# Taps of the last chunk on two DMA queues, step sizes and the sine's table first, and new figures for the order of the work: a gated attention and state-space kernel

## The chip, the cores and the metric

The kernel runs on one core of a Trainium2 chip. The core has a matmul engine (TensorE, PE in the profile), an engine for functions by table (ScalarE, ACT), a vector engine (VectorE, DVE), a general engine (GpSimd, POOL), and SyncE (SP), which here only starts DMA transfers. Each engine works through its own list of instructions in order and waits on semaphores that others raise. The metric is the time of one execution on the device in microseconds, the median of the runs.

## The reference

Two branches read the same x (2048 rows of 448), and a gate per row mixes them:

```python
g = sigmoid((x * gate_w).sum(-1, keepdims=True))
# A: attention with 16 query heads of 28, one key head and one value head
scores = einsum("bhqd,bkd->bhqk", q, k) * (28 ** -0.5)
a = einsum("bhqk,bkd->bhqd", softmax(scores), v) ... @ wo
# B: a long convolution with taps from 256 complex modes per channel
dt = exp(log_dt)[:, None]
P = exp(dt * (A_re + 1j*A_im) * l)            # l = 0..2047
K = einsum("dn,dnl,dn->dl", Cc, P, dt * Bc).real
b = causal_convolution(x, K) + x * Dskip      # by FFT in the reference
return g * a + (1 - g) * b
```

## The kernel before, in words

**Attention.** The 16 groups of work (four query blocks of 512 rows by four groups of four heads) each meet 16 key blocks, which makes 1024 score tiles of 128x512. They are taken in sets of three and two by turns: TensorE writes scores into PSUM (L1289 by row groups of 29, L1312 with a zero-padded query in qM; in the last 64 tiles L1300 and L1303), ScalarE takes one exponential over the set (L1344), and TensorE multiplies by the values (L1362, L1356). After each group the sums are copied out (L1127), the denominators go through DRAM, and four output projections per query block (L1109) are folded into O (L1118). For the last query block the end is different: two halves, each with a matmul that adds O through the identity (L1209), four projections (L1205) and a copy (L1226, L1223) before its store.

**Convolution.** The 448 channels are taken in 14 chunks of 32. For each, VectorE builds powers of the modes in a table by doubling (products L950, sums and differences L965, the closing products L979, a sign L986), TensorE turns the table into taps (L1009, two halves of a chunk), VectorE copies each half to `kstg` (L1019), and four DMAs on GpSimd's queue write it to DRAM (`KP_scratch`). SyncE loads the taps back as a Toeplitz pattern (`T`, four DMAs per eight channels), TensorE convolves (L1071), VectorE weights by 1-g (L1080), TensorE turns the result (L1091), and VectorE adds it to O (L1100). The input u of the convolution is rearranged from O's memory once, by 16 GpSimd copies (L598), and then shifted by DMAs.

**The start.** x comes in four blocks (`lx`) on SyncE's queue. Each block is transposed on TensorE (L639), copied from PSUM by ScalarE or VectorE (L649, L653), and multiplied by the key weights (L661); ScalarE writes kT (L673). The step sizes `log_dt` are one row, loaded on ScalarE's queue as the second DMA, spread over the partitions by a matmul with ones (L768), and taken through the exponential (L770), which is ordered behind the first copy of x. A dummy sine (L678) brings the sine's table in after the third block's copy; two real sines (L798, L799) and a dummy exponential (L800) follow.

**What sets the order.** A planner in the kernel's Python (`Prog.schedule`) places every operation by a planned duration in nanoseconds, a priority `pr` (smaller goes first among those that are ready), and the ends of what it depends on. It writes one order for each engine, and that order is what the chip follows. Durations are written at each operation: `el(n, rate)` is 68 + n/rate. `LAZY` adds a margin to matmuls of certain priorities; `PORT` holds VectorE for 0.55 of a long GpSimd operation. Transfers have planned costs too (`DMA_NS`, `iss`, `extra`). `pg.after` adds an order without data.

The planned durations of the exponentials, the table products and the folds are these:

```python
AF.Exp, scale=SQ), 58 + 512 * n / 1.2, rd=bk, wr=ew, pr=0)      # L1346, n = 3 or 2
def vo(fn, n, rd, wr, rate=1.92): ... el(n, rate)               # L930
ALU.mult, ALU.add), el(n), ...                                  # L1118, rate 0.96
```

Of the kernel before, what the change touches and what calls it, by code (L numbers as in the profile page):

```python
# [12 lines left out]
P = 128  # L13

S = 2048
D = 448
# [26 lines left out]
GATE = (30, 35)  # L43
WARM = 64
NEWQ = 15
STORES = (401, 405, 408)
# [38 lines left out]
class Prog:  # L85
# [12 lines left out]
    LAZY = {1.2: 200.0, 1.4: 200.0, 1.55: 200.0, 1.6: 200.0}  # L98
# [303 lines left out]
class Kernel:  # L402
# [75 lines left out]
    def consts(self):  # L478
# [21 lines left out]
        for k in range(2):  # L500
            pm(V(self.qM, k * XQ, XQ), 0.0, 1800, [("qM", k)], 1.5)
# [15 lines left out]
    def loads(self):  # L517
# [12 lines left out]
        def lraw(k, eng="sp"):  # L530
# [5 lines left out]
        lx(0)  # L536
        pg.dma([(wks.v(0, DT, 0, [[1, 112]]), dram(ins["A_wk"], 0, [[112, DT], [1, 112]]))], (112, 224), "wk", wr=["wks"], eng="act")
        pg.dma([(self.dtb.v(0, 1, 0, [[1, D]]), dram(ins["B_log_dt"], 0, [[D, 1], [1, D]]))], (1, 896), "ldt", wr=["dt"], eng="act")
        lx(1)
        pg.dma([(wks.v(0, DT, 112, [[1, 112]]), dram(ins["A_wv"], 0, [[112, DT], [1, 112]])),  # L540
                (wks.v(0, DT, 224, [[1, 4]]), dram(ins["gate_w"], 0, [[4, DT], [1, 4]]))],
               (224, 200), "wv", wr=["wvs"], eng="act", extra=1500)
# [4 lines left out]
               (112, 3584), "wq", wr=["wqs"], fac=0.85)  # L547
        lraw(1)
# [5 lines left out]
              180, rd=["wvs"], wr=["Wv"], pr=0.1)  # L554
        pg.op("dve", lambda e: e.tensor_copy(self.Wv.v(0, DT, 28, [[32, 4]]), wks.v(0, DT, 224, [[1, 4]])),
              100, rd=["wvs"], wr=["Wvg"], pr=0.1)
# [28 lines left out]
    def prep_u(self):  # L585
        pg = self.pg
        done = []
        for half in range(2):
            for k in range(2):
                for j in range(0, 8, 2):  # L590
                    jj = 8 * k + j
                    if half == 0:
                        dst, w = self.U.v(0, P, 2 * jj, [[128, UA // 2], [1, 4]]), ["Uz", ("Ub", k)]
                    else:
                        dst, w = self.T.v(0, P, UB + 2 * jj, [[32, UA // 2], [1, 4]]), ["rawdone", ("UB", k)]
                    key = ("ustd", half, jj)
                    done.append(key)
                    pg.op("pool", lambda e, dst=dst, jj=jj, half=half: e.tensor_copy(  # L598
                        dst, self.O.v(0, P, jj * D + half * UA, [[2, UA // 2], [D, 2], [1, 2]])), 660,
                        rd=[("ust", k)] + ([] if half else []), wr=w + [key], pr=1 + half)  # L600
# [23 lines left out]
    def prep_x(self):  # L624
# [6 lines left out]
        for q in range(4):  # L631
            for hp in range(2):
# [15 lines left out]
                if hp == 0 or q == 3:  # L648
                    o = pg.op("act", lambda e, d=dst, s=src: e.activation(d, s, AF.Copy), 1000, rd=[("b", b)], wr=[key])  # L649
                    if q == 0:  # L650
                        self.xc0 = o.i
# [802 lines left out]
```

## Time and profile before

| | us |
|---|---|
| median of 3 runs | 502.0 (500.86 to 503.79) |
| the profiled execution | 503.36 |
| its span, first to last instruction | 501.5 |
| ScalarE busy | 485.0 |
| PE busy | 468.2 |
| VectorE busy | 455.7 |
| GpSimd busy | 166.5 |

The span is what the profile's rows cover; the profiled execution's time is 1.9 us longer. A row of the timeline gives start, duration, engine, line, operation, the tiles written and read, and in brackets the idle time before it and what ended it. Neighbouring instructions of a kind are merged, and the first form is the one shown. Instructions on one engine overlap by about 0.1 us, so the distance between two starts is what one costs. A wait's three numbers are the total, the count and the longest. Line numbers are those of the kernel before.

### The profile page before, as it was taken

Reading aid. Unit: us, or ns where it says so; the run is one execution under the profiler, and the core shown is the slowest. Engines: PE = TensorE matmul, PEld = TensorE weight load, DVE = VectorE, ACT = ScalarE, POOL = GpSimd, SP = SyncE. Lnnn points to the kernel's source line nnn. Section 1 sums busy time; section 2 is a strip of 40 time slices with the busy share of each in tenths; the row PEclk is TensorE's granted clock in tenths of the full one; section 3 lists DMA queues with packets and bytes.
Section 4 is the critical chain, followed back from the end, with each engine's and each line's share of the span. In section 5 each row is a group of like instructions: output and inputs, shape, how many; then the busy total and the mean of one; then the engine's idle time right before and its main releaser. Section 6 shows DMA issues by size and latency. Waiting matters only on the chain.

```text
span 501.5 us, 17468 instructions
## 1 busy us (share of the span) xinstructions
PE 468.2 (93%) x7651; PEld 213.7 (43%) x7734; DVE 455.7 (91%) x862; ACT 485.0 (97%) x435; POOL 166.5 (33%) x308
## 2 busy tenths in 40 slices
PE   8899999999999999989999999988999999999997
PEld 6532233344443334444443434434444253455563
DVE  5999999999999999999999999989999999994222
ACT  5999999999999999999999999989999999999995
POOL 5106534233243243224316124521512540535110
PEclk9799999999999999999999999989999999999999
DMA  8997289847519348995934861799692666777942
GB/s 236 324 190 191 26 189 132 274 118 241 158 25 284 102 125 208 276 242 114 272 87 104 237 180 46 225 250 263 175 255 36 195 205 182 218 204 209 298 153 78
DMA packets 151527, 91.86 MB, mean 183 GB/s; under 512 B 83514, under 2 KB 147436, under 8 KB 151452
## 3 DMA queue, kind: packets, MB, share of 16 engines
q1 hardware_dynamic: 141962, 81.05, 60.2%
q0 software_dynamic: 8960, 9.54, 7.8%
q8 instruction: 60, 0.98, 0.8%
q10 hardware_dynamic: 530, 0.17, 0.2%
q14 instruction: 15, 0.12, 0.1%
HBM read 73.61 MB, written 5.23 MB: 157 GB/s over the span
## 4 chain that ended last, share of the span: by engine, by line
DVE 57%; ACT 23%; PE 16%; DMA 2%; issue 1%; SPq 0%
ACT expT L1344 22%; DVE tab L950 19%; DVE tab L965 10%; DVE tab L979 4%; DVE tmp L973 3%; DVE msq L896 3%; PE psS L1289 2%; DVE kstg L1019 2%; PE psB L1362 2%; PE psS L1312 2%; DVE cst L1080 2%; DMA T<-KP_scratch 1%; DVE seedz L898 1%; DVE mbf L916 1%; DVE acc L1127 1%; DVE qT L869 1%
## 5 line engine op out<-in xcount | busy, mean ns | idle before, releaser
L1344 ACT ACTIVATE expT<-psS 128x1536 bf16<-128x1536 f32 (+1 forms) x410 | 466.2, 1326 | 4.6 <-PE psS L1289 2.8
L950 DVE TENSOR_TENSOR tab<-tab,mbf 128x512 bf16<-128x512 bf16 (+4 forms) x140 | 140.4, 1007 | 0.0
L1289 PE MATMUL psS<-qT,kT 29*128 29x512 bf16 x654 | 92.2, 387 | 8.1 <-ACT expT L1344 4.0
L1362 PE MATMUL psB<-expT,vaug 128*32 128x512 bf16 x960 | 96.1, 391 | 0.4 <-DVE acc L1127 0.3
L151 POOL DMA_DIRECT2D KP_scratch<-kstg x112 | 61.6, 557 | 101.5 <-DVE kstg L1019 101.0
L1312 PE MATMUL psS<-qM,kT 128*128 128x512 bf16 x234 | 76.1, 383 | 11.8 <-issue 8.1
L965 DVE TENSOR_TENSOR tab<-tab 128x256 bf16<-128x256 bf16 (+4 forms) x140 | 78.6, 585 | 0.0
L1362 PEld LDWEIGHTS psB<-expT,vaug 128*32 128x32 bf16 x960 | 24.6, 93 | 70.6 <-issue 68.8
L1271 PE MATMUL psB<-ident,one 128*128 128x512 bf16 x168 | 53.9, 383 | 0.1
L151 POOL DMA_DIRECT2D qM<-qT x64 | 32.6, 515 | 58.5 <-DVE qT L869 37.2
L1289 PEld LDWEIGHTS psS<-qT,kT 29*128 29x128 bf16 x654 | 22.6, 91 | 55.9 <-ACT expT L1344 40.8
L151 POOL DMA_DIRECT2D rdenB<-R_scratch x60 | 30.3, 510 | 48.1 <-DMA R_scratch<-denT 48.0
L1071 PE MATMUL psS<-T,U 128*26 128x128 bf16 (+3 forms) x1792 | 40.0, 223 | 0.7 <-DMA T<-KP_scratch 0.7
L1071 PEld LDWEIGHTS psS<-T,U 128*26 128x26 bf16 (+3 forms) x1792 | 31.6, 106 | 15.0 <-issue 9.6
L1071 PE MATMUL psX<-T,U 128*32 128x128 bf16 (+3 forms) x1472 | 33.8, 222 | 1.5 <-issue 1.2
L979 DVE TENSOR_TENSOR tab<-tab,tmp 128x1984 bf16<-128x1984 bf16 x28 | 32.6, 1188 | 0.1
L1071 PEld LDWEIGHTS psX<-T,U 128*32 128x32 bf16 (+3 forms) x1472 | 25.4, 106 | 14.1 <-issue 10.9
L1312 PEld LDWEIGHTS psS<-qM,kT 128*128 128x128 bf16 x306 | 18.8, 97 | 26.6 <-ACT expT L1344 17.0
L973 DVE TENSOR_TENSOR tmp<-tmp,mq 128x64 bf16<-128x64 bf16 (+4 forms) x70 | 26.1, 373 | 0.2
L1271 PEld LDWEIGHTS psB<-ident,one 128*128 128x128 bf16 x168 | 15.2, 97 | 23.0 <-issue 13.1
L896 DVE TENSOR_TENSOR msq<-seedz 128x512 f32<-128x512 f32 (+1 forms) x40 | 24.9, 622 | 0.0
L151 POOL DMA_DIRECT2D R_scratch<-denT x15 | 8.5, 565 | 48.1 <-DVE denT L1133 20.1
(186 smaller groups left out, 522.3 us busy)
## 6 DMA issues: line engine op xcount, KB each, us to landing
T<-KP_scratch SPq DMA_DIRECT2D x204, 272.0 KB, 5.0
U<-KP_scratch SPq DMA_DIRECT2D x20, 272.0 KB
rdenB<-R_scratch POOLq DMA_DIRECT2D x60, 64.0 KB
U<-cst SPq DMA_DIRECT2D x1, 3584.0 KB, 23.8
qM<-qT POOLq DMA_DIRECT2D x64, 32.0 KB, 4.6
tab<-in_A_x_dram SPq DMA_DIRECT2D x4, 448.0 KB, 6.1
O<-in_A_x_dram SPq DMA_DIRECT2D x16, 112.0 KB, 2.9
O<-cst SPq DMA_DIRECT2D x1, 1792.0 KB, 10.6
```

The costliest lines, as they stand in the source:

```text
L151: return [e.dma_start(o, i, **kw) for o, i in pairs]
L896: pg.op("dve", lambda e: e.tensor_tensor(m2(msq), z2, z2, ALU.mult), el(2 * n), rd=[kr, ki] + first, wr=["msq"], pr=pr)
L950: mul = lambda e, o, a, b: e.tensor_tensor(o, a, b, ALU.mult)
L965: vo(lambda e, dv=dv, tv=tv, k=k: e.tensor_tensor(dv, dv, tv, ALU.add if k else ALU.subtract), n, [kt[k], kd[k]], [kd[k]])
L973: vo(lambda e, w=w, lv=lv: e.tensor_tensor(rho.v(0, P, (32 - 2 * w) * 2, [[64, 32], [2, w], [1, 2]]), rho.v(0, P, (32 - w) * 2, [[64, 32], ...
L979: vo(lambda e, k=k: e.tensor_tensor(tab.v(0, P, FM + k * FP + 2, [[64, 32], [2, 31], [1, 2]]), tab.v(0, P, lm + k * PL + 62, [[64, 32], [- ...
L1071: r = e.matmul(ps.v(32 * j, 32 - m0, 128 * k, [[1, 128]]), self.U.v(0, P, (4 * gi + j) % UA // 2 * 128 + 2 * (2 * m0 + par) + j % 2, [[4, ...
L1271: return e.matmul(t.v(0, P, off, [[1, 512]]), self.one.v(0, P, 2, [[0, P]]), self.ident.v(0, P, 0, [[0, 4], [1, P]]), start=b != 6, stop=b ...
L1289: r = e.matmul(self.psS.v(0, P, 512 * b, [[1, 512]]), kT.v(32 * h, DH + 1, 128 * kt, [[1, 128]]), qT.v(32 * h, DH + 1, 512 * (i % 2), [[1, ...
L1312: return e.matmul(self.psS.v(0, P, 512 * b, [[1, 512]]), kT.v(0, P, 128 * kt, [[1, 128]]), self.qM.v(0, P, (i % 2) * XQ + 512 * h, [[1, 51 ...
L1344: pg.op("act", lambda e: e.activation(expT.v(0, P, 512 * es[0], spread(es, n)), self.psS.v(0, P, 512 * bs[0], spread(bs, n)), AF.Exp, scal ...
L1362: r = e.matmul(self.psB.v(32 * h, 32, 0, [[1, 512]]), vaug.v(0, P, 32 * kt, [[1, 32]]), expT.v(0, P, 512 * ring[t], [[1, 512]]), start=(kt ...
```

## The change

It has these parts.

- The last chunk (c = 13, `LASTQ`): the four DMAs that write the first half's taps go on SyncE's queue, with a semaphore slot of their own; the second half's stay on GpSimd's.
- The step sizes are the first DMA on ScalarE's queue, ahead of the key weights. The loads of the value and gate weights go from ScalarE's queue to SyncE's, behind the query weights. The step sizes' exponential is no longer ordered behind the first copy of x, and the dummy sine is ordered behind that exponential.
- The two memsets of qM go from GpSimd to VectorE (priority 1.5 to 0.5).
- u is rearranged by four VectorE copies of 32-bit pairs, in place of 16 GpSimd copies.
- The 18 warm-up matmuls write to another PSUM bank.
- Planned figures: the exponential 46 + 428 n; the first doubling's products at a rate of 1.09 and its sums at 1.16; the fold at 0.86. Priorities: the tap matmuls 1.4 to 1.15, the output projections 1.2 to 1.58 (with their keys in `LAZY`), the first transposes of the raw parameters 0 to -0.5, the product that follows 0.2 to -0.1, and the copies of the value weights 0.1 to 0.3.
- Which copies of x run on VectorE is now a table (`XDVE`) that names the same three. `TAFTER` is empty and orders nothing.

```diff
-    LAZY = {1.2: 200.0, 1.4: 200.0, 1.55: 200.0, 1.6: 200.0}
+    LAZY = {1.15: 200.0, 1.55: 200.0, 1.58: 200.0, 1.6: 200.0}
...
-            pm(V(self.qM, k * XQ, XQ), 0.0, 1800, [("qM", k)], 1.5)
+            dm(V(self.qM, k * XQ, XQ), 0.0, 1130, [("qM", k)], 0.5)
...
         lx(0)
+        pg.dma([(self.dtb.v(0, 1, 0, [[1, D]]), dram(ins["B_log_dt"], ...))], (1, 896), "ldt", wr=["dt"], eng="act", extra=-1500)
         pg.dma([(wks.v(0, DT, 0, [[1, 112]]), dram(ins["A_wk"], ...))], (112, 224), "wk", wr=["wks"], eng="act")
-        pg.dma([(self.dtb.v(0, 1, 0, [[1, D]]), dram(ins["B_log_dt"], ...))], (1, 896), "ldt", wr=["dt"], eng="act")
         lx(1)
-        pg.dma([(wks.v(0, DT, 112, [[1, 112]]), dram(ins["A_wv"], ...)), ...], (224, 200), "wv", wr=["wvs"], eng="act", extra=1500)
...
+        pg.dma([(wks.v(0, DT, 112, [[1, 112]]), dram(ins["A_wv"], ...)), ...], (224, 200), "wv", wr=["wvs"], extra=1500)
...
+        U4, T4, O4 = (b.cast(mybir.dt.int32) for b in (self.U, self.T, self.O))
...
-                    pg.op("pool", lambda e, dst=dst, jj=jj, half=half: e.tensor_copy(
-                        dst, self.O.v(0, P, jj * D + half * UA, [[2, UA // 2], [D, 2], [1, 2]])), 660, ...
+                pg.op("dve", lambda e, dst=dst, k=k, half=half: e.tensor_copy(
+                    dst, O4.v(0, P, (8 * k * D + half * UA) // 2, [[1, UA // 2], [D // 2, 8]])), 1000, ...
...
-            if q == 2:
-                pg.op("act", ... AF.Sin), 1340, rd=["hpi", ("xT", 0, 2)], wr=["dum"], pr=-3)
...
         o = pg.op("act", lambda e: e.activation(d1, pl(), AF.Exp), 500, rd=["ldx"], wr=["dt"], unlock=L)
-        pg.after[o.i] = self.xc0
+        d = pg.op("act", ... AF.Sin), 1340, rd=["hpi"], wr=["dum"], pr=-3)
+        pg.after[d.i] = o.i
...
-        p0, k0 = trans(0, 0)
+        p0, k0 = trans(0, -0.5)
...
-                   2 * n, done[0] + done[1][2:] + mk(lv), [kd[k], kt[k]] + late)
+                   2 * n, done[0] + done[1][2:] + mk(lv), [kd[k], kt[k]] + late, 1.92 if lv else 1.09)
...
-            pg.dma(lst, (512, 128), f"kw{q}", rd=[("kst", q)], wr=[("KP", c, q)], pr=0, eng="pool", extra=1800)
+            if c < LASTQ or q in LASTP:
+                pg.dma(lst, (512, 128), f"kw{q}", rd=[("kst", q)], wr=[("KP", c, q)], pr=0, eng="pool", extra=1800)
+            else:
+                o = pg.dma(lst, (512, 128), f"ks{q}", rd=[("kst", q)], wr=[("KP", c, q)], pr=0, iss=700.0)
...
-                                                AF.Exp, scale=SQ), 58 + 512 * n / 1.2, rd=bk, wr=ew, pr=0)
+                                                AF.Exp, scale=SQ), 46 + 428 * n, rd=bk, wr=ew, pr=0)
```

## The prediction

> **What bounds the kernel now.** I read the busy table first, then ScalarE's waits, its timeline, and last the two ends. From the page, the busy line, the exponentials' group, the chain by engine:
>
> ```profile
> PE 468.2 (93%) x7651; PEld 213.7 (43%) x7734; DVE 455.7 (91%) x862; ACT 485.0 (97%) x435; POOL 166.5 (33%) x308
> ...
> DVE 57%; ACT 23%; PE 16%; DMA 2%; issue 1%; SPq 0%
> ...
> L1344 ACT ACTIVATE expT<-psS 128x1536 bf16<-128x1536 f32 (+1 forms) x410 | 466.2, 1326 | 4.6 <-PE psS L1289 2.8
> ```
>
> ScalarE is busy 485.0 of 501.5 us, 466.2 of it on exponentials that no part of the change touches. The chain names VectorE more often only because it is followed through in-order work; VectorE is free from about 455 us on. So time can be won only where ScalarE stands still: before its stream, inside it, after it. ScalarE's waits, and rows of its timeline:
>
> ```profile
> ACT O L1223 <- PE psS L1205: 3.8, 1, 3.8
> ACT expT L1344 <- PE psS L1289: 2.8, 6, 0.9
> ...
> ACT xT L649 <- PE psS L639: 2.3, 1, 2.3
> ACT expT L1344 <- PE psS L1312: 1.1, 2, 0.9
> ...
> 6.24 1.02 ACT L649 ACTIVATE xT<-psS 112x1024 bf16<-112x1024 bf16 x1 [2.29 <-PE psS L639]
> 7.16 0.54 ACT L770 ACTIVATE cst<-psX 128x448 bf16<-128x448 f32 x1
> ...
> 10.66 1.28 ACT L678 ACT_TABLE_LOAD   x1
> ...
> 349.02 28.14 ACT L1344 ACTIVATE expT<-psS 128x1024 bf16<-128x1024 f32 x25
> ...
> 344.29 150.44 ACT L1344 ACTIVATE expT<-psS 128x1024 bf16<-128x1024 f32 x133 [0.87 <-PE psS L1312]
> ```
>
> The stretch at 349 us is nearly clean: 28.14/25 = 1.126 us per exponential. The timeline's rows from 31.47 us to the end of the last exponential (494.73) hold 404 of them in 463.3 us. At the clean rate they take 454.9, so 8.4 us are lost inside the stream: 3.8 as idle rows, the rest in handoffs too short for a row. Of the idle rows 0.92+0.23+0.72+0.87 = 2.7 us lie at 329-345 us, where the granted clock is 0.86 (325-332).
>
> The last chunk and the end:
>
> ```profile
> 453.39 0.69 DVE L986 TENSOR_SCALAR tab<-tab 128x2048 bf16<-128x2048 bf16 x1
> ...
> 456.29 0.69 DVE L1019 CAST kstg<-psX 128x512 bf16<-128x512 f32 x1 [1.87 <-PE psX L1009]
> ...
> 457.27 2.20 POOL L151 DMA_DIRECT2D KP_scratch<-kstg  x4 [1.34 <-DVE kstg L1019]
> ...
> 462.35 9.68 SPq L151 DMA_DIRECT2D T<-KP_scratch  x12
> ...
> 489.47 0.42 DVE L1100 TENSOR_TENSOR O<-O,psX 128x256 bf16<-128x256 bf16 x1 [0.54 <-PE psX L1091]
> ...
> 490.44 0.36 PE L1209 MATMUL psS<-O,ident 128*128 128x448 bf16 x1
> ```
>
> The last convolution is added to O by 489.89 us, 4.8 us before the exponentials end. What follows (495.3 to 498.5) hangs on attention, not on this.
>
> **The sum's base.** The profiled execution took 503.36 us: span 501.5 and 1.9 around it. That is 1.4 above the median of 502.0; I work out differences and apply them to the median.
>
> **Part 1, the start.** Two operations leave the middle of ScalarE's start: the step sizes' exponential L770 (7.16 to the next start 7.58 = 0.42) and the sine's table load with its dummy (10.66 to 12.06 = 1.40). They go ahead of the first x copy. Their gate is L768, which needs the step sizes, issued first now, and `one`. VectorE writes `one` behind the two qM memsets that come over from GpSimd. A uint32 memset of 128 elements takes 0.17 us and one of 32 takes 0.09, so 1024 words are about 0.95 us; GpSimd's 1.81 is the other bound. GpSimd, without them, builds the identity earlier, which ends the first idle stretch. Two of 0.95 fit the idle stretches of VectorE (1.87 until 3.55, 1.95 until 5.66), so `one` stands at about 4 us. The Wk copy, which waits for its DMA until 5.66, is planned behind `one`. The plan puts L768 behind 17 of 18 warm-up matmuls (0.21 each from 1.14), so it ends near 5.1; the exponential starts at 5.2, and the first x copy at 5.2+0.5+1.28+0.1 = 7.1, not 6.24. ScalarE works 1.04 us earlier.
>
> It then waits more. The first L661 group (1.04) starts when that copy ends at 8.1, so kT can start at 9.2, and ScalarE is ready at 9.0: 0.2 idle. The transposes of the raw steps (L781, 0.56) now have priority over the second L661: 9.2+0.54+0.56+1.04 = 11.4 against ScalarE ready at 10.8: 0.6. The table load used to cover exactly this. The last quarter's transposes give 0.5, the sine's argument 0.25. That is 1.55 us of waits, against 0.43+0.16+0.16 = 0.75 before. Net -1.04+0.80 = **-0.2 us**. Bounds: -1.0, if the waits do not grow, and +1.5, if half of the 1.40+0.42 that covered waits turns into waiting and L768 holds the x transposes by 0.7. The first exponential may come 1 to 2 us later; that costs nothing where L804 and the five L807 (0.95 and 0.97 each), ScalarE's own work, go ahead of it. The two weight loads moved from ScalarE's queue (0.33+0.44) to SyncE's delay the raw loads behind them by 0.9: the second, issued at 4.16, lands after 9.1 us, and is used at 19.46. Hidden; 0.9 if its transposes come forward.
>
> **Part 2, u on VectorE.** Removed: 16 GpSimd copies between 43 and 56 us (12.0 us of GpSimd). Added: four VectorE copies of 128x896 words. [...] GpSimd's copies slow VectorE now:
>
> ```profile
> 42.13 0.29 DVE L900 TENSOR_TENSOR seedz<-msq 128x128 f32<-128x128 f32 x1
> ...
> 42.45 0.29 DVE L916 CAST mbf<-seedz 128x256 bf16<-128x256 f32 x1
> ...
> 43.81 0.59 DVE L900 TENSOR_TENSOR seedz<-msq 128x128 f32<-128x128 f32 x1
> ...
> 44.50 0.66 DVE L916 CAST mbf<-seedz 128x256 bf16<-128x256 f32 x1
> ```
>
> About 15 VectorE instructions lose 0.3 us each: 4.6 us come back. VectorE: -0.3; on the path 0, under the slack of part 4. [...]
>
> **Part 3, new figures and priorities.** The planner writes the order of every engine, and TensorE serves it strictly, so a matmul whose VectorE input is late holds the score matmuls behind it. VectorE was planned too short: the 128x256 L950 starts 0.31 after the one before, was planned at 0.20, now at 0.30; the 128x128 L965 0.18, planned 0.135, now 0.178; the fold L1118 0.60, planned 0.535, now 0.589. Over 28, 28 and 12 instructions that is 2.9+1.2+0.65 = 4.7 us. The exponentials are planned shorter: 1.116 a piece, not 1.125, 3.4 us over 404. Both move VectorE's results later against the exponentials, so fewer are unfinished when TensorE comes to them. The tap matmuls rise above the projections (1.15 and 1.58, from 1.4 and 1.2): one more reason for the last chunk to come earlier, without a row of its own. The nearest row is 169.74 us, where L1091 waited 0.52 for VectorE and the next exponential 0.53. Of the 8.4 us lost I leave out the 2.7 at 329-345 (clock) and take a third of the remaining 5.7: **-1.9 us**. Bounds: -5.7, and +3.6, the 2.7 again and the 0.9 of handoffs, if new places stall.
>
> **Part 4, the last chunk.** The first half's four stores move from GpSimd (2.20 us of issue) to SyncE, which is idle from 454.07 to 462.35. Four issues at the 0.6 of its T loads are 2.5; landing is 3.0 after issue for SyncE's only store of kstg, 2.3 by the median of GpSimd's. From the cast's end (456.98) to T's loads are 5.4 now, and 0.1+2.5+2.3 to 3.0 = 4.9 to 5.6 after: between -0.5 and +0.2 us. Behind the waiting store stand only the T loads that need it and the output stores. The second half's stores were not held by the first's (459.47 to 460.41 is idle). [...] The written order itself moves the last chunk, relative to the exponentials' end: +3.4 +4.7 +4.0 of planned copies -5.8 of planned GpSimd blocking (16 x 0.55 x 0.66) = 6.3 us later. Against the slack of 4.8 plus what follows I charge **+0.2 us**; bounds 0 and +3.
>
> Sum: -0.2-1.9+0.2 = -1.9, so 502.0-1.9 = **500.1 us**, and 501.5 for a profiled run like the one shown.
>
> **Rivals.** (a) *The new figures fit almost everywhere.* The whole 5.7 us of waits goes: 502.0-0.2-5.7+0.2 = 496.3; with most of it 497. For: the planned durations now are the rows' own. Against: the tap matmuls (L1009) stay planned at 0.25 per 16 matmuls, and TensorE stays 93% busy. (b) *Slower: the last chunk falls out of cover.* Place: L1209 waits for the last add. Two tiles of half 0, ten matmuls at 0.22, must be through before L1205 at 497.3, so it decides once the add ends after about 494. A slide of 6.3 puts it at 496.2: +1.2 to +1.5; one of 8, +3: 504.8. Against: TensorE serves the last scores by 493.3 and is free after. (c) *Slower: a second stretch at half clock.* TensorE's granted clock is 0.69 at 20-30 us and 0.86 at 325-332. One more such stretch in the stream costs what that at 329-345 does, 2.7 idle and 0.9 around it: 502.0+3.6-0.2 = 505.4. For: TensorE waits more in the new start. [...] (d) *The start does not do what it says:* L768 behind `one` and the waits at their bound, +1.5, with part 3 at a third: 501.8.
>
> **How the numbers follow.** Mine 0.38 (own range 498.5 to 502); (a) 0.32; (b) 0.12; (c) 0.10; (d) 0.08. Half a per cent, 2.5 us, is about what a measurement can tell here: (a) is faster, mine and (d) the same, (b) and (c) slower. The range 496.3 to 505.2 leaves out about one tenth at each end.
>
> **What would show it.** Right: L770 and the sine's load before the first x copy, near 7.1 us; no slow VectorE rows at 43-56; fewer L1344 idle rows outside a half-clock stretch; T loads at about 5 us behind the cast. Wrong: L768 after 6 us; the last L1100 after 494; more than 10 us lost against 1.126 per exponential.

## The result and the profile after

The changed kernel takes 508.06 us (median of four executions, 506.70 to 510.10) against 502.32 for the kernel before (four executions too). The ratio is 1.0115, with a 95% interval of 1.0088 to 1.0142, so it is slower by about 1.1%. The prediction was 500.1 us with a range of 496.3 to 505.2, so it was wrong in sign and in range. The profiled execution took 508.98 us, its span is 507.2.

The busy line, the chain by engine and the group of the exponentials, from the page of the changed kernel (lines have moved: the exponentials are L1351 now, the set-wise score matmuls L1296 and L1319, the tap matmuls L1010, their copies L1020, the last adds L1107, the end's matmuls L1216 and L1212):

```profile
PE 480.6 (95%) x7718; PEld 213.6 (42%) x7718; DVE 457.2 (90%) x868; ACT 484.5 (96%) x435; POOL 147.8 (29%) x286
...
ACT 76%; PE 17%; DMA 3%; DVE 2%; issue 1%; SPq 1%
...
L1351 ACT ACTIVATE expT<-psS 128x1536 bf16<-128x1536 f32 (+1 forms) x410 | 465.1, 1392 | 8.5 <-PE psS L1296 4.1
```

ScalarE does the same work as before (484.5 us busy against 485.0). It only waits longer: 8.5 us ahead of exponentials, where it was 4.6. The chain names ScalarE now, since its stream and not VectorE's in-order work is followed back. GpSimd has lost 18.7 us of its work. PE's busy time is 12 us higher, which I don't read further, since the two traces hold different numbers of its matmuls. ScalarE's waits by name:

```profile
ACT O L1230 <- PE psX L1212: 6.5, 1, 6.5
ACT expT L1351 <- PE psS L1296: 4.1, 8, 0.9
ACT expT L1351 <- PE psS L1319: 3.2, 5, 1.2
```

The first is the end: ScalarE's one output copy waits 6.5 us for the last projections, where it was 3.8.

To see where the 5.7 us lie I cut the span of each profile at two points: the start of the twenty-first exponential, and the end of the last one. What follows the second point I call the tail.

| us | before | after | difference |
|---|---|---|---|
| start of the 21st exponential | 47.54 | 50.32 | +2.78 |
| from there to the end of the last | 447.19 | 447.61 | +0.42 |
| tail | 6.75 | 9.26 | +2.51 |
| span | 501.5 | 507.2 | +5.7 |

**The start.** Rows of ScalarE's and TensorE's timeline, after:

```profile
7.00 1.00 ACT L652 ACTIVATE xT<-psS 112x1024 bf16<-112x1024 bf16 x1
...
19.98 2.62 ACT L808 ACTIVATE mq<-T 128x896 bf16<-128x896 f32 x3
23.01 2.37 ACT L1351 ACTIVATE expT<-psS 128x1536 bf16<-128x1536 f32 x2 [0.41 <-PE psS L1296]
...
30.42 1.45 ACT L1351 ACTIVATE expT<-psS 128x1536 bf16<-128x1536 f32 x1 [0.87 <-PE psS L1296]
...
34.10 2.37 ACT L1351 ACTIVATE expT<-psS 128x1536 bf16<-128x1536 f32 x2 [0.81 <-PE psS L1319]
...
20.85 0.61 PE L867 MATMUL psX<-qT,Wb 128*128 128x512 bf16 x1 [1.62 <-DVE Wb L697]
```

The same place in the kernel before:

```profile
19.35 2.37 ACT L1344 ACTIVATE expT<-psS 128x1536 bf16<-128x1536 f32 x2 [0.16 <-PE psS L1289]
...
22.50 1.80 ACT L807 ACTIVATE mq<-T 128x896 bf16<-128x896 f32 x2
...
17.96 0.66 PE L684 MATMUL psB<-expT 112*128 112x29 bf16 x20 [1.21 <-DVE Wb L698]
```

And the view by windows of about 3.4 us, first before, then after (columns: the window; its length; busy time and count of PE, PEld, DVE, ACT, POOL; granted clock of TensorE; DMA share; GB/s):

```profile
26.19:29.60 3.41, 3.41 (x23) 1.17 (x23) 3.41 (x4) 3.41 (x5) 0.00 (x0) 1.00 1.11 285
...
27.24:30.66 3.42, 3.42 (x19) 1.12 (x16) 3.42 (x5) 2.55 (x4) 0.78 (x1) 0.50 1.05 263
```

The first copy of x starts at 7.00, as predicted (7.1). The first exponential comes at 23.01 instead of 19.35. In between ScalarE does its own work early: three of the five mode exponentials (`mq`) and the exponential of the real parts stand ahead of the stream; before, all six stood behind its first exponentials. Then it waits for scores at 23, 30, 32 and 34 us: between the first exponential and the twenty-first it is idle for 2.32 us, before for 0.16. TensorE itself was late. `Wb` is a matrix that VectorE makes from maxima over the keys, and that TensorE multiplies with the queries' maxima before the first scores. It was finished at 20.80, before at 17.68; TensorE waited 1.62 us for it, before 1.21. Then TensorE's clock was at half from 20.41 to 30.66, before from 19.36 to 26.19.

**The end.** Rows of the last chunk and of what follows, after:

```profile
465.86 0.69 DVE L1020 CAST kstg<-psS 128x512 bf16<-128x512 f32 x1 [4.16 <-PE psS L1010]
...
466.58 2.61 SPq L155 DMA_DIRECT2D KP_scratch<-kstg  x4
470.31 5.65 SPq L155 DMA_DIRECT2D T<-KP_scratch  x8
...
499.82 0.42 DVE L1107 TENSOR_TENSOR O<-O,psS 128x256 bf16<-128x256 bf16 x1
...
500.40 0.36 PE L1216 MATMUL psX<-O,ident 128*128 128x448 bf16 x1
```

The last table ends at 458.67 (454.09 before), 4.6 us later; the first half's taps reach `kstg` at 466.55 (456.98), 9.6 later, because VectorE's copy waits 4.16 us for tap matmuls that stand later in TensorE's order. SyncE's store then does what it was meant to: 3.76 us from the copy's end to the T loads, 5.4 before. The last add ends at 500.25 and the exponentials at 497.93. Before, the add was 4.84 us ahead of that point; now it is 2.31 behind, and L1216 starts right after it.

### The profile page after: what moved, and what is told of

Same layout as the page of the kernel before. It is cut to its first block, busy times and chain, and to the rows that moved or that the text cites. A ratio compares the mean times of both kernels' runs of the same rounds, so it can differ in the third digit from the quotient of the medians.

```text
span 507.2 us, 17500 instructions
## 1 busy us (share of the span) xinstructions
PE 480.6 (95%) x7718; PEld 213.6 (42%) x7718; DVE 457.2 (90%) x868; ACT 484.5 (96%) x435; POOL 147.8 (29%) x286
## 4 chain that ended last, share of the span: by engine, by line
ACT 76%; PE 17%; DMA 3%; DVE 2%; issue 1%; SPq 1%
ACT expT L1351 75%; DMA T<-KP_scratch 3%; PE psS L1319 2%; PE psS L1296 2%; PE psX L1078 2%; PE psB L1369 1%; PE psS L1310 1%; PE psS L1078 1%; PE psB L1363 1%; PE psS L632 1%; PE psB L1272 1%; PE psS L1010 1%; PE psS L1307 1%; SPq L155 1%; PE psB L1278 1%
## 5 line engine op out<-in xcount | busy, mean ns | idle before, releaser
L1351 ACT ACTIVATE expT<-psS 128x1536 bf16<-128x1536 f32 (+1 forms) x410 | 465.1, 1392 | 8.5 <-PE psS L1296 4.1
L1296 PE MATMUL psS<-qT,kT 29*128 29x512 bf16 x654 | 92.5, 391 | 11.7 <-ACT expT L1351 7.4
L1319 PE MATMUL psS<-qM,kT 128*128 128x512 bf16 x306 | 93.0, 387 | 1.3 <-ACT expT L1351 1.1
L155 POOL DMA_DIRECT2D KP_scratch<-kstg x108 | 59.1, 554 | 75.4 <-DVE kstg L1020 71.5
L966 DVE TENSOR_TENSOR tab<-tab 128x256 bf16<-128x256 bf16 (+4 forms) x140 | 77.4, 573 | 0.0
L1296 PEld LDWEIGHTS psS<-qT,kT 29*128 29x128 bf16 x654 | 22.5, 91 | 63.2 <-ACT expT L1351 52.5
L1078 PE MATMUL psX<-T,U 128*26 128x128 bf16 (+3 forms) x1920 | 45.5, 225 | 3.2 <-DMA T<-KP_scratch 2.1
L1278 PE MATMUL psB<-ident,one 128*128 128x512 bf16 x150 | 48.4, 384 | 0.0
L1078 PEld LDWEIGHTS psX<-T,U 128*26 128x26 bf16 (+3 forms) x1920 | 33.9, 107 | 20.1 <-issue 12.1
L155 POOL DMA_DIRECT2D denT<-acc x15 | 11.1, 740 | 104.0 <-DVE acc L1134 91.6
L1078 PE MATMUL psS<-T,U 128*32 128x128 bf16 (+3 forms) x1344 | 29.9, 221 | 0.1
L1319 PEld LDWEIGHTS psS<-qM,kT 128*128 128x128 bf16 x306 | 18.3, 97 | 27.5 <-ACT expT L1351 18.6
L1078 PEld LDWEIGHTS psS<-T,U 128*32 128x32 bf16 (+3 forms) x1344 | 23.0, 105 | 10.3 <-issue 7.2
L1010 PE MATMUL psS<-tab 128*64 128x128 bf16 x608 | 26.3, 224 | 0.0
```

The source lines that it names most:

```text
L155: return [e.dma_start(o, i, **kw) for o, i in pairs]
L966: vo(lambda e, dv=dv, tv=tv, k=k: e.tensor_tensor(dv, dv, tv, ALU.add if k else ALU.subtract), n, [kt[k], kd[k]], [kd[k]], 1.92 if lv else ...
L1010: r = e.matmul(G.v(64 * u, 64, 128 * k, [[1, 128]]), tab.v(0, P, lo + comp * PL + cg * 64 + u, [[2, 64]]), tab.v(0, P, fo, [[64, 2], [mo - ...
L1078: r = e.matmul(ps.v(32 * j, 32 - m0, 128 * k, [[1, 128]]), self.U.v(0, P, (4 * gi + j) % UA // 2 * 128 + 2 * (2 * m0 + par) + j % 2, [[4, ...
L1278: return e.matmul(t.v(0, P, off, [[1, 512]]), self.one.v(0, P, 2, [[0, P]]), self.ident.v(0, P, 0, [[0, 4], [1, P]]), start=b != 6, stop=b ...
L1296: r = e.matmul(self.psS.v(0, P, 512 * b, [[1, 512]]), kT.v(32 * h, DH + 1, 128 * kt, [[1, 128]]), qT.v(32 * h, DH + 1, 512 * (i % 2), [[1, ...
```

## The experiments

Sixteen kernels ran. Experiments 1 to 4, 5 to 8, 9 to 12 and 13 to 16 each shared a chip and the runs of the kernel before. A ratio is to these, with its 95% interval. "Start", "VectorE's figures" (first doubling 1.09 and 1.16, fold 0.86) and "the exponential's figure" name parts of the diff. Theory C in the first expectations is that the start and TensorE's clock cost the time, theory L that the last chunk has left the cover of the exponentials.

### 1. The start alone

```diff
+            dm(V(self.qM, k * XQ, XQ), 0.0, 1130, [("qM", k)], 0.5)
...
+        pg.dma([(self.dtb.v(0, 1, 0, [[1, D]]), dram(ins["B_log_dt"], ...))], (1, 896), "ldt", wr=["dt"], eng="act", extra=-1500)
...
+        d = pg.op("act", ... AF.Sin), 1340, rd=["hpi"], wr=["dum"], pr=-3)
+        pg.after[d.i] = o.i
...
+        p0, k0 = trans(0, -0.5)
```

These and the moved loads and the warm-up's bank are added to the kernel before.

> The kernel before with the new start alone (step sizes first, their exponential and the sine's table before the x copies, value weights on SyncE's queue, qM's memsets on VectorE, the warm-up bank, the first transposes' priority). Theory C (clock): the new order leaves TensorE waiting between 13 and 21 us, its clock stays at half for 10.2 us instead of 6.8, and the stream loses about 2.5 us: 504 to 505.5. Theory L (the last chunk leaves its cover) says this part does not matter: 501.5 to 503.

Measured: 504.84 us (10 executions) against 502.31; 1.0049 (1.0027 to 1.0070). The start costs 2.5 us by itself. The twenty-first exponential starts at 49.51, the tail is 6.84, close to the 6.75 before. The clock is at half for 6.8 us, not for the 10.2 that theory C names, but from 22.73 to 29.56, which ends 3.4 us later than before.

### 2. The planned figures alone

```diff
+                   2 * n, ..., [kd[k], kt[k]] + late, 1.92 if lv else 1.09)
+                   ... ALU.add if k else ALU.subtract), n, ..., 1.92 if lv else 1.16)
+                   el(n, 0.86), rd=rd + ["gt"], ...
+                   AF.Exp, scale=SQ), 46 + 428 * n, rd=bk, wr=ew, pr=0)
```

> The kernel before with the planned figures alone (exponentials 46+428n, first doubling at 1.09 and 1.16, folds at 0.86). Theory L: the written order moves the last chunk later against the exponentials' end, the last add to O ends after the exponentials, and the end grows by 3 to 6 us: 505 to 508. My prediction's part 3 says 500 to 501. Theory C says no effect at the end: 501 to 503.

Measured: 509.77 against 502.31; 1.0126 (1.0091 to 1.0161). The 21st exponential starts at 48.03, near the kernel before's, the last add ends 8.22 us behind the exponentials and the tail is 15.04, 8.3 us longer, where theory L named 3 to 6. One wait shows it, from ScalarE's waits of this kernel:

```profile
ACT O L1223 <- PE psS L1205: 12.3, 1, 12.3
```

The same copy waited 3.8 in the kernel before. So the figures that were to win time in the stream lost more than that in the last chunk.

### 3. The change without any new figure

```diff
-                                                AF.Exp, scale=SQ), 46 + 428 * n, rd=bk, wr=ew, pr=0)
+                                                AF.Exp, scale=SQ), 58 + 512 * n / 1.2, rd=bk, wr=ew, pr=0)
```

The other three lines of experiment 2 are taken back too.

> The changed kernel with the old planned figures. Theory L: the last add is back under the exponentials, the 2.5 us at the end and the stalls around 460 us go: 503.5 to 505.5. Theory C alone: 507 to 508.5.

Measured: 506.89; 1.0081 (1.0049 to 1.0113). The tail is back at 7.08, with the add 2.65 us ahead; the twenty-first exponential stays at 50.25. The time lies between the two readings: the tail's part came back, the start's did not.

### 4. The change with the old start

```diff
-        d = pg.op("act", ... AF.Sin), 1340, rd=["hpi"], wr=["dum"], pr=-3)
-        pg.after[d.i] = o.i
+        pg.after[o.i] = self.xc0
```

All lines of experiment 1 are taken back out of the changed kernel.

> The changed kernel with the old start. Theory C: the half clock at the start is back to 6.8 us and 2.5 us come back: 505 to 506. Theory L alone: 507.5 to 508.5.

Measured: 502.42 (10 executions); 0.9999 (0.9974 to 1.0025). Undoing the start takes away all that can be measured, more than either reading named, though the tail is still 9.13 in the profile. The rest of the change has to win about as much elsewhere. The profile, which is of the slowest of the ten executions (505.11), shows 0.9 us of it, in the stream (446.3 us against 447.2); where the rest comes from stays open, and the costs of the parts do not simply add up.

### 5. The start, with two of VectorE's products put behind Wb

The start alone (experiment 1) has on VectorE:

```profile
15.55 1.09 DVE L791 TENSOR_TENSOR T<-psX,cst 128x896 f32<-128x896 bf16 x1
...
19.03 1.09 DVE L791 TENSOR_TENSOR seedz<-tab,T 128x896 f32<-128x896 f32 x1 [0.38 <-ACT tab L803]
20.04 0.35 DVE L695 SCALAR_TENSOR_TENSOR Wb<-expT,small,Wb 128x128 bf16<-128x128 bf16 x1
```

In the kernel before, both products came after 20 us and the last instruction for `Wb` started at 17.32. The edit keeps that instruction's number as `self.wb`, and orders behind it TensorE's second raw transposes, which the first of the two products needs, and the second product itself.

```diff
+        self.wb = o.i
...
         p1, k1 = trans(1, 1)
+        pg.after[self.rawx] = self.wb
...
-        vt(zc(1), tc(5), tc(3), ALU.mult, ...)
+        pg.after[vt(zc(1), tc(5), tc(3), ALU.mult, ...)] = self.wb
```

> The new start alone (as in the run that added only the start, 504.8), with one thing put back: the second raw transposes (L780) and VectorE's third parameter product are ordered behind the last instruction that writes Wb. In the run with the start alone, two products of 1.0 us (L791 at 15.55 and 19.03) stand on VectorE ahead of Wb, which is finished at 20.4 instead of 17.7, and TensorE waits 1.62 for it. Theory V (VectorE's products delay Wb, and with it the first scores): Wb is finished near 18, the first score matmul starts near 19 instead of 21.6, the waits of the exponentials between 23 and 36 us shrink from 2.4 to below 1, and the time comes back by 1.5 to 2.5, to 502.3 to 503.3. Rival A (ScalarE's own work, five exponentials of the modes and one of the steps, was used up ahead of the stream, and TensorE's transposes pace the first twenty exponentials whenever they begin): the stream's twenty-first exponential does not come earlier by more than 0.5 and the time stays at 504.3 to 505.

Measured: 503.42 (10 executions) against 502.79; 1.0023 (0.9989 to 1.0058). From the same rows of this kernel:

```profile
17.81 0.35 DVE L695 SCALAR_TENSOR_TENSOR Wb<-expT,small,Wb 128x128 bf16<-128x128 bf16 x1
...
19.40 0.60 PE L1290 MATMUL psS<-qT,kT 29*128 29x512 bf16 x5 [0.29 <-DVE qT L870]
```

The first exponential is at 19.84, the twenty-first at 47.78 (47.54 before), and ScalarE does not wait for scores between 20 and 38 us. So what theory V says of `Wb`, of the scores and of the waits came, and rival A's forecast for the twenty-first exponential did not. The times alone would not tell the two apart, since the interval overlaps that of experiment 1 (1.0027 to 1.0070). The early load of the step sizes and the sine has no cost that this run can tell; the rows put the cost on their consumers, which are ready earlier and get in front of `Wb`. One thing the edit does not separate: with it all six of ScalarE's own operations stand behind the first exponential again (22.15 to 30.82), where experiment 1 has two of them.

### 6. The start without the raised priority

```diff
-        p0, k0 = trans(0, -0.5)
+        p0, k0 = trans(0, 0)
-        vt(tt(1), p0, dtp2, ALU.mult, [k0, "rd"], [K(1)], -0.1, unlock=p0)
+        vt(tt(1), p0, dtp2, ALU.mult, [k0, "rd"], [K(1)], 0.2, unlock=p0)
```

> The new start alone, but with the priority of the first raw transposes and of the product behind them as before (0 and 0.2 in place of -0.5 and -0.1). Theory V: the priority is what put VectorE's products ahead of Wb; without it Wb is ready before 18.5 us and the time is 502.3 to 503.5. Rival B: the early step sizes do that by themselves, because the products are ready earlier than they were; then Wb stays near 20 us and the time at 504.5 to 505.

Measured: 509.02; 1.0126 (1.0076 to 1.0177), worse than the start with it, which neither reading foresaw. The sine's argument now comes late (ScalarE waits 2.57 us for it, until 17.51), the last instruction for `Wb` starts at 18.75, TensorE's clock is at half for 10.2 us from 19.23, and the twenty-first exponential starts at 50.98, although all six own operations of ScalarE stand behind the first one (21.30); the stream takes 449.4 us, 2.2 more than before. So the priority by itself is not the fault: without it the sine's argument is the late one, and `Wb` still comes 1.4 us later than before.

### 7. The change with the last chunk's tap matmuls first

```diff
-                      wr=[(X, q), ("kst", q)], pr=1.15, lock=G if k == 0 else None)
+                      wr=[(X, q), ("kst", q)], pr=1.15 if c < 13 else -0.5, lock=...)
```

> The changed kernel with one priority altered: the tap matmuls of the last chunk go first (-0.5 in place of 1.15), nothing else. Theory L (the last chunk has left the cover of the exponentials: the last add ends 2.3 us behind them and the tail has grown from 6.8 to 9.3): the cast of the first half no longer waits 4.2 us for its tap matmuls, the last add ends 2 to 4 us earlier, the tail falls to 7 to 8, and the time to 506 to 507 from 508.1. Rival T (the tail is held by attention's last projections, not by the convolution): the casts come earlier, but the tail stays at 9 and the time at 508.

Measured: 507.34; 1.0114 (1.0077 to 1.0151). The taps reach `kstg` at 461.94, 4.6 us earlier, the last add ends 0.54 behind the exponentials instead of 2.31, and the tail is 8.65 instead of 9.26. The direction is theory L's, the size is smaller: the add moves by 1.8 us where it named 2 to 4, the tail shrinks by 0.6 where it named 1.3 to 2.3, and the time itself cannot be told from the change's.

### 8. Old start, VectorE's old figures, taps first

```diff
-                      wr=[(X, q), ("kst", q)], pr=1.15, lock=G if k == 0 else None)
+                      wr=[(X, q), ("kst", q)], pr=1.15 if c < 13 else -0.5, lock=...)
...
-        pg.after[d.i] = o.i
+        pg.after[o.i] = self.xc0
...
-                   el(n, 0.86), ...
+                   el(n), ...
```

These lines are against the changed kernel. The whole start and all three of VectorE's figures are as before.

> The changed kernel with the start as before, VectorE's planned figures as before, and the last chunk's tap matmuls first: what stays of the change is the copies of u on VectorE, SyncE's store of the first half, the planned figure of the exponential and the two other priorities. If theory L and the start's cost are all that made the change slower, nothing is lost at either end (tail near 6.8, first exponential at 19.5), the stream keeps what it has of gains, and the time is 500 to 502, the same as before or a little faster. If the stream itself is worse by the new order, it is 503 or more.

Measured: 508.92; 1.0122 (1.0063 to 1.0181). Both ends are good (21st exponential at 46.95, tail 6.68). The stream took 452.9 us instead of 447.2. Three stops of TensorE, each followed by a stretch at half clock, hold 9.35 us of the loss. One of them in the view by windows, cut at the changes of the clock:

```profile
363.12:366.53 3.41, 3.34 (x50) 1.04 (x38) 3.41 (x5) 3.41 (x4) 1.84 (x4) 1.00 0.81 203
366.53:369.94 3.41, 1.52 (x10) 0.41 (x10) 3.41 (x3) 3.13 (x3) 0.00 (x0) 1.00 1.06 304
369.94:373.36 3.42, 3.39 (x73) 1.96 (x74) 0.84 (x2) 1.00 (x1) 0.00 (x0) 0.50 1.12 363
373.36:376.77 3.41, 3.41 (x56) 1.47 (x54) 3.41 (x6) 3.41 (x4) 0.00 (x0) 1.00 0.90 197
```

In the second window TensorE was busy for 1.52 us; it waited 1.91 for a T load. The whole next window ran at half clock. Of its four executions the one with the highest clock (0.99) took 503.91, the others (0.983 to 0.987) 508.4 to 509.6.

### 9. The change with VectorE's old figures

```diff
-                   2 * n, ..., 1.92 if lv else 1.09)
+                   2 * n, ...)
-                   ... n, [kt[k], kd[k]], [kd[k]], 1.92 if lv else 1.16)
+                   ... n, [kt[k], kd[k]], [kd[k]])
-                   el(n, 0.86), ...
+                   el(n), ...
```

> The changed kernel with VectorE's planned figures (first doubling, its sums, the fold) as before, all else as changed. Theory L: these longer figures are what moved the last chunk out of the exponentials' cover; without them the last add ends 3 us or more ahead of the exponentials' end, the tail is 6.7 to 7.1 in place of 9.3, and the time 505 to 506, the start's cost remaining. Rival: the exponential's shorter figure does it; then the tail stays above 8 and the time at 507 to 508.

Measured: 504.26 against 501.92; 1.0047 (1.0025 to 1.0070). The last add is 3.38 us ahead of the exponentials' end, the tail 6.90, and ScalarE's wait at the end is short again:

```profile
ACT O L1230 <- PE psX L1212: 4.1, 1, 4.1
```

Theory L holds. VectorE's longer figures moved the last chunk; without them the change costs what the start alone costs (1.0049 in experiment 1).

### 10. Filler matmuls ahead of the matmul with Wb

```diff
+        kap = len(pg.ops) - 1
...
+        for k in range(7):
+            o = pg.op("pe", ... matmul(self.psS.v(0, P, 4 * 512, [[1, 256]]), ...), 213,
+                      rd=[("cst", 1)], wr=["warm", ("b", 4)], pr=-0.5)
+            pg.after[o.i] = kap
```

`kap` is the number of VectorE's operation that takes the maximum which `Wb` is made from.

> The changed kernel with seven more warm-up matmuls (0.21 us each) written ahead of the matmul with Wb, where TensorE stands still for 1.62 us (19.23 to 20.86) before its clock drops for 10.2 us. They compute nothing that is used. Theory C (the gap lowers the clock, and the low clock stretches TensorE's preparation and the first exponentials' waits): the half-clock stretch at 20 us goes or shrinks to 3.4 or 6.8, and 1 to 2 us come back, to 506 to 507. Rival V (VectorE's late results alone pace the start): the clock may rise, but the twenty-first exponential comes at 50.3 as now, and the time stays at 508.

Measured: 506.45; 1.0095 (1.0058 to 1.0131). The edit did not do quite what it was meant to: the fillers ran at 17.77 and a gap of 1.78 us stayed behind them. But the stretch at half clock shrank from 10.2 to 3.4 us, and the four executions have mean clocks of 0.993 to 1.000, the changed kernel's four 0.983 to 0.990. The first exponential is at 22.08, only 0.9 earlier than in the change, yet the twenty-first starts at 47.87, 2.4 earlier. Experiments 1 and 7 have the first exponential at 22.09 too, with 6.8 us at half clock in place of 3.4, and their twenty-first comes at 49.51 and 49.30, 1.4 to 1.6 later. So, as far as kernels with different orders can show it, the low clock delays the first exponentials once ScalarE has little else to do. The tail is 9.44 and stays in the time. Since order and gap both changed, this run alone would not separate clock from order; the next table does more.

Start of the 21st exponential against the end of the first stretch at half clock, for the old start and the new one (the starts of experiments 5, 6, 11 and 12 are neither, and one profile has no such stretch):

| start | end of the stretch: start of the 21st exponential |
|---|---|
| old start | 25.2: 46.95 (exp. 8); 25.7: 47.18 (exp. 14); 26.0: 47.33 (exp. 15); 26.2: 47.54 (before); 26.6: 47.83 (exp. 13); 26.7: 47.91 (exp. 4); 27.1: 48.03 (exp. 2) |
| new start | 26.1: 47.87 (exp. 10); 28.2: 48.79 (exp. 9); 29.1: 49.30 (exp. 7); 29.6: 49.51 (exp. 1); 30.6: 50.25 (exp. 3); 30.7: 50.32 (the change) |

In both rows a later end by 1 us costs about 0.55 us, and where the rows overlap (26.1 and 26.2) the new start is worse by 0.4. So of the 2.78 us lost by the twenty-first exponential, some 2.4 go with the stretch ending 4.5 us later. The end of the stretch is not all: in experiment 6 it ends at 29.5, and the twenty-first exponential (50.98) comes 1.5 us later than the new start's row would have it.

### 11 and 12. With the start mended: u alone, and the rest

```diff
+        pg.after[self.rawx] = self.wb
...
+                pg.op("dve", lambda e, dst=dst, k=k, half=half: e.tensor_copy(
+                    dst, O4.v(0, P, (8 * k * D + half * UA) // 2, [[1, UA // 2], [D // 2, 8]])), 1000, ...
```

Both have the edit of experiment 5. The first (these lines) adds only u's four VectorE copies to the start alone; the second is the whole change with VectorE's old figures (experiment 9) and the taps first (experiment 7).

> The start alone with the repair behind Wb (503.4), and u's four copies on VectorE besides, nothing else of the change. The prediction's part 2 says: copies of 1.0 us each come in, 4.6 us of slowed VectorE rows at 43 to 56 us go, nothing on the path. So the rows at 43 to 56 are 0.29 again, the table of the last chunk ends within 1 us of where it did, and the time is the same, 502.5 to 504. Rival: VectorE's relief lets the stream lose less, and the time falls below 502.

Measured: 505.45 against 501.92; 1.0072 (1.0037 to 1.0107).

> The changed kernel with three repairs: the second raw transposes and the third parameter product behind Wb (which took the start's cost from 2.5 to 0.6 us), VectorE's planned figures as before, and the last chunk's tap matmuls first. If the start and the last chunk are all that the change loses, both ends are as before (first exponential near 19.8, last add 4 to 5 us ahead of the exponentials' end, tail 6.8), and the rest (u on VectorE, the exponential's figure, priorities, SyncE's store) shows its own worth: 500 to 502.5 against 502.5. If new written orders bring new stops of TensorE inside the stream, as the run with the old start and the taps first had them (5.7 us in the stream), it is 504 or more.

Measured: 506.44; 1.0095 (1.0063 to 1.0127).

With u alone, the last table ends at 450.59 (451.26 in experiment 5), so VectorE gains 0.7 us, where part 2 says 0.3 and its expectation within 1. The time missed the expectation, though the interval overlaps that of experiment 5; its seven executions run from 502.49 at a clock of 0.993 to 508.80 at 0.986, and the profile loses 6.8 us of its stream in eleven stops of over 0.3 us, experiment 5's 4.8 in eleven. That the copies cause them is not shown. The second kernel has both ends of the kernel before (47.62 and a tail of 6.69) and is still slower by its median, so the stream itself is worse, as the second reading of its expectation says. The profile is of its fastest execution (504.01) and has no stretch at half clock inside: eight stops hold 7.3 us, four of them of 0.8 to 1.7.

### 13 to 16. The exponential's figure alone, and three orders with the old start

```diff
-                                                AF.Exp, scale=SQ), 58 + 512 * n / 1.2, rd=bk, wr=ew, pr=0)
+                                                AF.Exp, scale=SQ), 46 + 428 * n, rd=bk, wr=ew, pr=0)
```

This line is the whole of the first. Each of the last three is the change with the old start and the taps first. They differ in which of VectorE's figures is the old one: the first doubling's products, its products and sums, or the fold.

> The kernel before with one line of the change: the exponential planned as 46 + 428 n. In the profiles so far, the four orders written with this figure and VectorE's new ones lose 2.5 to 3.1 us in small handoffs (0.06 to 0.3 us each, 20 to 23 places) after the twenty-first exponential, outside half-clock stretches; orders with the old figure lose 3.5 to 4.7 at 25 to 38 places, the kernel before 4.74 at 34. Theory E (the exponential's figure does it): at most 25 places and 3.2 us here, and the time 500 to 502 with the last add within 1 us of the exponentials' end. Rival D (VectorE's figures do it): 30 places or more, and the time 502 to 503.5.

Measured: 503.59 (10 executions) against 502.30; 1.0023 (0.9997 to 1.0049). Losses of 0.06 to 0.3 us: 3.9 us at 26 places. The last add ends 1.39 us ahead of the exponentials' end, 3.5 later than before.

> The changed kernel with the start as before, the last chunk's tap matmuls first, and of VectorE's planned figures only the first doubling's products back at the old one. The planner's order then has the last add ahead of the exponentials' end by some 2 us, so the tail should be 6.7 to 7.5. If a written order with the shorter exponential and no slipped last chunk is all it takes, the time is 500 to 501.5, less than before; if stops of TensorE in the stream come with every new order, it is 502.5 or more.

Measured: 504.47 (10 executions); 1.0022 (0.9990 to 1.0055). Tail 6.90, 14.5 us lost in the stream.

> As the run before it, with the first doubling's sums at the old figure too (only the fold and the exponential keep the new ones). Tail 6.7 to 7 with more room. The same two readings: 500 to 501.5 if only the last chunk and the start were wrong with the change, 502.5 or more if new orders bring stops. Three such orders that differ in one figure each show how far the stops depend on the order alone.

Measured: 502.52 (10 executions); 0.9990 (0.9962 to 1.0018). Tail 6.76, 8.2 us lost in the stream, the shortest span of all profiles (498.0).

> As the two before it, but with only the fold at the old figure; the first doubling's products and sums keep the new ones. Tail 6.8 to 7.5. The same two readings: 500 to 501.5, or 502.5 and more.

Measured: 503.42 (10 executions); 1.0012 (0.9986 to 1.0037). Tail 7.08, 13.2 us lost in the stream.

The exponential's figure alone falls between its two readings and settles neither. None of the three orders is faster or slower than the kernel before by what can be measured. Their streams differ by 6 us in the profiles, but each profile is of one execution, and the ten executions of each order spread over 4.5 to 6.1 us, so the profiles do not rank the orders. No version found beats the kernel before.

## Why the prediction was wrong, point by point

**Part 1 (-0.2, bounds -1.0 to +1.5): wrong; 2.5 by the run with it alone.** Its times for the first copy of x and for ScalarE's early work were right (7.00 against 7.1), and so were the waits ahead of the stream (0.63, 0.22, 0.21 and 0.59, together 1.65; 1.55 was summed). The step that failed is that a later first exponential "costs nothing where L804 and the five L807 (0.95 and 0.97 each), ScalarE's own work, go ahead of it". The first exponential came 3.7 us later, and four of those six went ahead of it, but it was not free: ScalarE's idle time between the first exponential and the twenty-first, which the sum has at nothing, was 2.32 us in place of 0.16. The cause that the runs show is that TensorE's preparation of the first scores was late and ran longer at half clock. The prediction followed the transposes that come forward only on TensorE, and not the products behind them on VectorE, which stood in front of `Wb`. With `Wb` finished at 18.17 and 3.4 us at half clock the idle time is 0.02 (experiment 5); with `Wb` as late as in experiment 1, but 3.4 us at half clock, it is 0.92 (experiment 10; 2.44 in experiment 1). That the work spent early had been the cover for this is likely, since the waits follow it, but not shown apart: experiment 5 puts it back together with `Wb`, and experiment 6, which has all of it behind the first exponential, waits 1.56 us all the same.

**Part 2 (0 on the path): its rows were right.** Rows of VectorE after:

```profile
44.41 0.28 DVE L901 TENSOR_TENSOR seedz<-msq 128x128 f32<-128x128 f32 x1
...
46.98 0.95 DVE L601 COPY U<-O 128x896 int32<-128x896 int32 x1
```

A copy takes 0.95 to 0.97 us. The forecast's -0.3 on VectorE is four copies at 1.08 (4.3 us) against the 4.6 that come back; 1.08 is the time of L796 before, and 0.62, that of L795, was the other bound, both of other operations on 128x896 float32. No run shows a copy at either time. The product that took 0.59 beside GpSimd's copies takes 0.28 again. That the path neither gains nor loses is not settled: experiment 11, with the copies alone, ends its last table 0.7 us earlier and measures 1.0072 where experiment 5 has 1.0023, with intervals that overlap.

**Part 3 (-1.9): not there; +0.4.** The handoffs did shrink in this pair: after the twenty-first exponential, outside stretches at half clock, losses below 0.3 us sum to 5.9 us before and 4.1 after (counted against 1.331 us from the start of a three-tile exponential to the next and 0.904 for two, the spacing of undisturbed ones; by this count the stream before lost 11.5 us, where the prediction found 8.4 with 1.126 for each). What the sum left out as fixed, the 2.7 us around a half-clock stretch, did not stay fixed: the changed kernel's profile has two such stretches in its stream (215.0 and 460.7 us) with 5.2 us around them, against one with 2.5. Over all profiles, the twelve orders with the exponential's new figure lose 3.2 us on average in places of 0.06 to 0.3 us, the six with the old one 4.1; but the whole loss of the stream is 12.1 against 11.8. The step that failed is to count the smaller handoffs as won while all other stops stay as they were: what the handoffs gain comes back in stops of over 0.3 us. These sums are of one execution for each order. That an order can make the stream itself worse is shown by the times of experiments 8 and 12, which have both ends as before and are slower by 1.0122 and 1.0095; why one order has more stops than another stays open.

**Part 4 (+0.2, bounds 0 and +3): mis-sized; +2.5.** The slide of 6.3 us against a slack of 4.8 was nearly right: the last add went from 4.84 ahead to 2.31 behind, 7.15 us. The step that failed is the charge, 0.2 for an overrun that the text itself had worked out, on the ground that TensorE is free after 493. The gain of SyncE's store was larger than its bounds (1.6 us; -0.5 to +0.2 had been given), and was lost before it counted, in the 4.16 us that the copy waits for the tap matmuls. The profiles of all kernels give the price of a late add, which was a bound only:

| last add against the exponentials' end | tail |
|---|---|
| -5.64 (experiments 11, 15), -4.84 (before; experiments 5, 6, 8, 12) | 6.7 to 6.8 |
| -4.42, -3.38, -3.36 (experiments 1, 9, 14) | 6.84, 6.90, 6.90 |
| -2.65, -2.54, -1.39 (experiments 3, 16, 13) | 7.08, 7.08, 7.35 |
| +0.54 (experiment 7) | 8.65 |
| +1.30, +2.31, +2.50 (experiment 4, the change, experiment 10) | 9.13, 9.26, 9.44 |
| +8.22 (experiment 2) | 15.04 |

The add begins to cost about 3 us ahead of the exponentials' end, earlier than the rival's "after about 494", which is 0.7 ahead.

**The rivals.** (b), the last chunk, and (c), the clock, were both on the slower side and were priced at 2.8 and 3.4 us above the kernel before. They got 0.12 and 0.10 as alternatives; both came, together. (c) came mostly at the start; the profile has one more such stretch in the stream too, but the stream as a whole lost only 0.4 us. Its ground, that TensorE waits more in the new start, was there (1.62 us for `Wb`, 1.21 before), and the table in the last section has the falls to half clock behind windows in which TensorE was less busy. (d) had the right place, but stopped at +1.5, and L768 was not held: its exponential starts at 5.04. Nothing speaks for (a).

## What to carry to other kernels

Work that an engine does early is no gain if what it then waits for is not ready earlier too: ask of each moved piece what the engine will do in the place where it used to stand, and of each operation that becomes ready earlier what it will now stand in front of. Where a planned order slides a chain past the end of its cover, charge the overrun in full. A new written order can draw new stops, so a few tenths won at every handoff are not to be counted on until the order has been seen on the chip.

## What the runs showed of the hardware

All changes of TensorE's granted clock in one profile lie on a grid of 3.413 us. In the kernel before they come at 19.36, 26.19, 329.97, 333.39 and 500.64 us, which are 2, 89, 1 and 49 steps apart; in the change the steps are 3, 54, 1, 71, 1 and 13. The stretches at half clock last 3.4, 6.8 or 10.2 us, but for the last one, which the end cuts off. In the 18 profiles the clock fell from full to half only behind windows of the grid in which TensorE was less than 0.80 busy. From the rows of matmuls, without the last windows of each profile, which the end cuts off:

| busy share of a window at full clock | windows | next at half clock |
|---|---|---|
| below 0.55 | 12 | 12 |
| 0.55 to 0.65 | 27 | 14 |
| 0.65 to 0.80 | 78 | 4 |
| above 0.80 | 2439 | 0 |

In experiment 8 the stops of 1.90, 1.91 and 2.09 us were each followed by a window at half clock. In the change a stop of 1.31 us for a T load (213.59 to 214.90), in a window 0.61 busy, was followed by one; a stop of 1.24 us (491.84 to 493.08), in a window 0.64 busy, was not. Such stretches may be one reason why executions of one kernel differ; that is not shown. The kernel before has 78 executions beside these experiments: the 16 with a mean clock below 0.9915 average 504.2 us, the 43 between that and 0.9945 average 502.0, and the 19 above it 502.4.
